# Weights laid out on the host in load order, raw w1 blocks loaded from there, and b2 added by matmuls, in a two-layer transformer block on one core

## The chip, the core and the metric

The kernel runs on one core of a Trainium2 chip. The metric is device time in microseconds (us) of one execution. The core has a matrix engine (TensorE, in profiles PE for matmuls and PEld for weight loads), VectorE (DVE), ScalarE (ACT), GpSimd (POOL) and SyncE (SP), which here only issues DMAs. Every engine takes its instructions in order; they meet through semaphores. Sixteen DMA engines carry all transfers, whichever engine issued them.

## The reference

x has 2048 tokens of 1024 numbers, in bfloat16. Two layers are computed, each an attention part and a feed-forward part with the same weights in both layers:

```python
x = A_x
x = x + _A_ref(_layernorm(x), A_wqkv, A_wo)
x = x + _B_ref(_layernorm(x), B_w1, B_b1, B_w2, B_b2)
x = x + _A_ref(_layernorm(x), A_wqkv, A_wo)
x = x + _B_ref(_layernorm(x), B_w1, B_b1, B_w2, B_b2)
```

_A_ref is attention with 32 heads of 32, in which token s looks at the eight tokens s, s-2, ..., s-14, between a product with wqkv (1024 x 3072) and one with wo (1024 x 1024). _B_ref is h = x w1 + b1 (w1 is 1024 x 3584), h = max(h, 0) squared, out = h w2 + b2 (w2 is 3584 x 1024).

## The kernel before

**Units.** Tokens are sorted into even and odd ones, so that the dilated window becomes a window of eight neighbours. A layer has four blocks of 512 tokens; with two layers these are units u = 0 to 7. For each unit the stages are: SA (load of x, LayerNorm, transposed to xnA), SQ (q, k, v: products `pq` of 8 matmuls of 512 columns each), S2 (window attention on VectorE, with matmuls `lg` and exponentials on ACT), SW (product with wo, `py`, residual `xm`, second LayerNorm to xnB), SF1 (x w1, bias, squared ReLU into `r2`) and SF2 (r2 w2, bias b2, residual, store). Between the layers the residual goes through the DRAM tensor xs, in bfloat16. `build` lists the stages of unit u beside SA, SQ and S2 of unit u + 1.

**The plan.** Nothing is issued as it is listed. Every operation goes into a list with its engine, a guessed duration, a priority and the tiles it reads and writes; `schedule` walks a model of the engines and fixes the order in each engine's queue. Tiles come from slots in size classes (8K: nine slots, among them at most six weight tiles `w`). The operations of `setup` are not in the plan: they are issued first.

**The start.** `setup` makes constants with memsets on VectorE and selects on GpSimd, and loads b1 as b1T (L259) and b2 broadcast to 128 partitions as b2b (L261) by DMAs that GpSimd issues. `build` puts 11 matmuls on constants on TensorE (L1005), which nobody reads. Unit 0's LayerNorm (`ln_first`) runs as statistics on VectorE (L518, L519), two small ACT steps (L522, L523), normalisation on VectorE (L526), transposes on TensorE (L539) and copies out of PSUM on ACT and VectorE (L542). The first products need four x tiles and the k weights, then the q weights: six loads of 1 MB in the order k, k, q, q, v, v. The order of TensorE there is three half products of k on tiles 0 and 1 (L605), one whole one of k, the first one of q (L600), and so on.

**Fast products.** Unit 0 does its feed-forward part plainly (SF1_plain, SF2_plain). Meanwhile it builds what units 1 to 7 use: there both products are cut into 2 x 2 blocks and done with seven block products instead of eight. Some products take sums or differences of blocks of w1 and w2. `keep_w1` and `keep_w2` make those on VectorE and store them in DRAM tensors w1s and tw. The seven products of a step of SF1 take four made blocks (products 3, 5, 6, 7) and three raw ones (1, 2, 4). `copy_w1` copies the raw ones, 21 blocks of 256 KB, from w1 into w1s, DRAM to DRAM, each waiting for one of unit 0's products, so that w1s holds all 49 blocks in the order of use. SF1 then reads w1s in loads of four blocks (1 MB), and treats a raw block's bits as bfloat16.

**b2.** b2 is put into PSUM banks before the products add to them: `seed` lets ACT copy b2b, or the difference b2d of its halves, into a bank (L373): eight banks in unit 0, two X and two Z banks in each of the other units. b2d is made by one VectorE subtraction (L1021) which `build` lists behind S2 of unit 0; it reads nothing that the plan makes, and the plan put it first in VectorE's queue:

```
L586 Memset v
L1021 TensorTensor b2d<-b2b 128x512
L518 BNStats st<-x_110 128x6 x2
```

**Rows in DRAM.** The loads take slices of the weights as the host gave them: wqkv in rows of 2 KB (1024 of 3072 columns), w1 in SF1_plain in rows of 512 B, w2 blocks in SF2 in rows of 1 KB, w2 in SF2_plain in rows of 2 KB.

Of the kernel before, what the change touches and what calls it, by code (L numbers as in the profile page):

```python
# [43 lines left out]
class Buf:  # L44

    __slots__ = ("cls", "tag", "shape", "dt", "left", "slot", "tile", "idx", "seeded")
    count = {}

    def __init__(self, cls, tag, shape, dt):
        self.cls, self.tag, self.shape, self.dt = cls, tag, shape, dt  # L50
        self.left, self.slot, self.tile = 0, None, None
        self.seeded = False
        self.idx = Buf.count[tag] = Buf.count.get(tag, -1) + 1
# [7 lines left out]
class Plan:  # L61
# [45 lines left out]
    def schedule(self):  # L107
# [13 lines left out]
        unset = set(free["ps"])  # L121
# [3 lines left out]
        while left:  # L125
            progress = False
            for e in engs:
# [26 lines left out]
                for b in o.bufs:  # L154
                    if b.slot is None:
                        b.slot = free[b.cls].pop(0)
                        if b.cls == "ps":
                            if b.seeded and b.slot in unset:
                                raise RuntimeError("no product has set the bank of a seeded tile")
                            (unset.add if b.tag == "pt" else unset.discard)(b.slot)  # L160
                        live[b.tag] = live.get(b.tag, 0) + 1
                        placed[b.tag] = placed.get(b.tag, 0) + 1
# [52 lines left out]
class _Kernel:  # L215
    def __init__(self, ctx, tc, x, wqkv, wo, w1, b1, w2, b2, out, n_layers=2):
        self.ctx, self.tc, self.nc = ctx, tc, tc.nc
        self.x, self.wqkv, self.wo, self.w1, self.b1, self.w2, self.b2, self.out = x, wqkv, wo, w1, b1, w2, b2, out
        S, D = x.shape[-2], x.shape[-1]
        self.S, self.D = S, D  # L220
        self.F = w1.shape[-1]
# [13 lines left out]
    def setup(self):  # L235
# [24 lines left out]
        self.b2b = const.tile([128, D], BF, name="b2b")  # L260
        nc.gpsimd.dma_start(self.b2b[:], self.b2.rearrange("(o d) -> o d", o=1).to_broadcast([128, D]))  # L261
        self.b2d = const.tile([128, BLK], F32, name="b2d")

        self.wqkv_v = self.wqkv.rearrange("(kt p) n -> p kt n", p=128)
        self.wo_v = self.wo.rearrange("(p c) n -> p c n", c=self.NCH)
        self.w1_v = self.w1.rearrange("(kt p) n -> p kt n", p=128)
        self.w2_v = self.w2.rearrange("(kt p) n -> p kt n", p=128)
# [4 lines left out]
        self.xs = [tc.dram_tile([self.S, D], BF, name=f"xs{l}") for l in range(self.n_layers - 1)]  # L272
# [4 lines left out]
        self.order1 = self.ffn1_order()  # L277
        self.w1s = [tc.dram_tile([128, min(4, len(self.order1) - i), 4, 256], F16, name=f"w1s{i // 4}") for i in range(0, len(self.order1), 4)]
# [5 lines left out]
        sizes = [("8Q", 3, 8304), ("8K", 9, 8192), ("4K", 12, 4096), ("r2", 1, KF * BLK * 2), ("2K", 8, 2048), ("1K", 9, 1024),  # L284
# [28 lines left out]
    def weights(self, ap, kt, wide=False):  # L313
        b = Buf("8K", "w", [128, 8, 512], BF)
        if wide:
            self.dma(lambda: b[:].rearrange("p (a b) n -> p a (b n)", a=4), lambda: ap, (), [(b, 0)], 1.05, name="w")
        else:
            self.dma(lambda: b[:, :kt, :], lambda: ap, (), [(b, 0)], kt * 0.131, name="w")
        return b

    def w2_block(self, k2, n2):
        h = self.KF // 2
        return self.w2_v[:, k2 * h:(k2 + 1) * h, n2 * BLK:(n2 + 1) * BLK]

    def keep_w2(self, j0, n, w):
# [3 lines left out]
        def raw(k2, n2):  # L329
            return w[:, k2, :n, n2 * BLK:(n2 + 1) * BLK]  # L330
# [9 lines left out]
    def SF2_plain(self, u):  # L340
# [6 lines left out]
        for tl, n2 in banks:  # L347
            self.seed(banks[tl, n2], lambda n2=n2: self.b2b[:, n2 * BLK:(n2 + 1) * BLK], st["ff"][-4])
        for j0 in range(0, h, 2):
            n = min(2, h - j0)  # L350
            w = Buf("8K", "w", [128, 2, 2, 2 * BLK], BF)
            for k2 in range(2):
                self.dma(lambda w=w, k2=k2, n=n: w[:, k2, :n], lambda k2=k2, j0=j0, n=n: self.w2_v[:, k2 * h + j0:k2 * h + j0 + n, :],
                         (), [(w, k2)], n * 0.262, name="w")
            for tl in range(4):
                for n2 in range(2):
                    def fm(tl=tl, n2=n2, w=w, j0=j0, n=n):
                        bank = banks[tl, n2]
                        for k2 in range(2):
                            for j in range(n):  # L360
                                nc.tensor.matmul(bank[:], r2[:, k2 * h + j0 + j, tl * 128:(tl + 1) * 128], w[:, k2, j, n2 * BLK:(n2 + 1) * BLK],  # L361
                                                 start=False, stop=(j0 + n == h and k2 == 1 and j == n - 1), skip_group_check=True)
                    self.pe(2 * n, fm, [(r2, (k2 * h + j0 + j, tl // 2)) for k2 in range(2) for j in range(n)] + [(w, 0), (w, 1)],
# [5 lines left out]
    def seed(self, bank, src, gate):  # L369


        bank.seeded = True
        self.p.add("ACT", act(512), lambda: self.nc.scalar.copy(bank[:], src()), [("b2d", 0)], [(bank, 0)], 0.5, after=[gate], name="seed")  # L373

    def w2_rhs(self, name, half):
# [9 lines left out]
        return self.weights(self.w2_block(k2, n2)[:, half * h:(half + 1) * h, :], h)  # L385

    def ffn1_order(self):

        out = [(0, 1), (1, 1)]
        for a in range(0, self.NDP, 2):  # L390
            steps = [d for d in (a, a + 1) if d < self.NDP]
            then = [(d, 1) for d in (a + 2, a + 3) if d < self.NDP]
            for pr in (5, 6, 2, 7):
                out += [(d, pr) for d in steps]
            out += then
            for pr in (4, 3):
                out += [(d, pr) for d in steps]
        return out

    def copy_w1(self, after):  # L400

        after = iter(after)
        for i, (dp, pr) in enumerate(self.order1):
            if pr in (1, 2, 4):
                gate = next(after)
                m, k = {1: (0, 0), 2: (0, 1), 4: (1, 1)}[pr]
                c0 = m * (self.F // 2) + dp * 256
                self.dma(lambda i=i: self.w1s[i // 4][:, i % 4], lambda k=k, c0=c0: self.w1_v[:, 4 * k:4 * k + 4, c0:c0 + 256],
                         (), [(("w1s", i // 4), i % 4)], 0.3, prio=1e5 + i, after=[gate], name="w1cp", cast=BF)

    def keep_w1(self, dp, w):

        nc, p = self.nc, self.p
        at = {pr: i for i, (d, pr) in enumerate(self.order1) if d == dp}
# [4 lines left out]
        def store(pr, src, r, cast=None):  # L419
            i = at[pr]  # L420
            self.dma(lambda: self.w1s[i // 4][:, i % 4], src, r, [(("w1s", i // 4), i % 4)], 0.26, prio=50.0, name="w1st", cast=cast, lat=4.0)
# [124 lines left out]
    def load_x(self, layer, t, after=(), prio=None, tag="xt"):  # L546
        x = Buf("2K", tag, [128, self.D], BF)
        src, r = (lambda: self.par_tile(self.x_par, t)), ()
        if layer:
            src, r = (lambda: self.xs[layer - 1][t * 128:(t + 1) * 128, :]), [(("xs", layer - 1, t), db) for db in range(2)]  # L550
        self.dma(lambda: x[:], src, r, [(x, 0)], 0.27, prio=-10.0 if prio is None else prio, after=after, name="x")
        return x, lambda: x[:]
# [16 lines left out]
    def SQ(self, u, jobs, order=None, split=0):  # L569
# [6 lines left out]
        cols = {"q": 0, "k": D, "v": 2 * D}  # L576
        offs = {"q": 0, "k": HALO, "v": HALO}
        ws = {}
        for nm in jobs:
            st[nm] = Buf("8Q", nm, [128, NCH, offs[nm] + BLK], F16)  # L580
            ws[nm] = [self.weights(self.wqkv_v[:, 4 * kh:4 * kh + 4, cols[nm]:cols[nm] + D], 8, wide=True) for kh in range(2)]
# [5 lines left out]
            else:  # L587
                src = self.state[u - 1]["halo" + nm]
                p.add("DVE", 0.18, lambda dst=dst, src=src: nc.vector.tensor_copy(dst[:, :, 0:HALO], src[:]),
                      [(src, 0)], [(dst, "h")], -50.0, name="halo")  # L590
        if order is None:
            order = [(nm, c0) for nm in jobs for c0 in range(NCH)]
        for nm, c0 in order:
# [3 lines left out]
            def fm(pq=pq, w=w, c0=c0):  # L597
                for kd in range(KD):
                    wv = w[kd // 4][:].rearrange("p (a b) n -> p a (b n)", a=4)
                    nc.tensor.matmul(pq[:], wv[:, kd % 4, c0:D:8], xnT[:, :, kd, :], start=(kd == 0), stop=(kd == KD - 1))  # L600
            if split:
                def fh(n2, pq=pq, w=w, c0=c0):
                    for kd in range(KD):
                        wv = w[kd // 4][:].rearrange("p (a b) n -> p a (b n)", a=4)
                        nc.tensor.matmul(pq[:, n2 * HB:(n2 + 1) * HB], wv[:, kd % 4, c0:D:8], xnT[:, 2 * n2:2 * n2 + 2, kd, :],  # L605
# [123 lines left out]
    def SW(self, u):  # L729
# [6 lines left out]
        wos = [self.weights(self.wo_v[:, 4 * g:4 * g + 4, :], KD, wide=True) for g in range(2)]  # L736
# [21 lines left out]
    def SF1_plain(self, u):  # L758
        nc, p = self.nc, self.p
        KD, KF, F = self.KD, self.KF, self.F  # L760
# [4 lines left out]
        st["ff"] = []  # L765
        for dp in range(self.NDP):
            w = Buf("8K", "w", [128, 2, 8, 256], BF)
            for m in range(2):
                self.dma(lambda w=w, m=m: w[:, m], lambda m=m, dp=dp: self.w1_v[:, :, m * (F // 2) + dp * 256:m * (F // 2) + (dp + 1) * 256],
                         (), [(w, m)], 0.6, name="w")  # L770
            for m in range(2):
                for a in range(2):
# [18 lines left out]
                    if dp or m:  # L791
                        st["ff"].append(self.pe(8, fm, [(xnT, i) for i in range(4)] + [(w, m)], [(ph, 0), (ph, 1)], name="ph"))
# [8 lines left out]
    def SF1(self, u):  # L801
# [6 lines left out]
        self.ff = st["ff"] = []  # L808
# [11 lines left out]
        for j, (d, pr) in enumerate(self.order1):  # L820
            if j % 4 == 0:
                n = min(4, len(self.order1) - j)
                spare = last and j % 8 == 0
                w = Buf("8Q" if spare else "8K", "wl" if spare else "w", [128, 4, 4, 256], F16)
                self.dma(lambda w=w, n=n: w[:, 0:n], lambda j=j: self.w1s[j // 4][:],
                         [(("w1s", j // 4), i) for i in range(n)], [(w, 0)], n * 0.24, after=[st["attended"]] if spare else (), name="w")
            if d not in steps:
                steps[d] = self.ffn1_step(r2, d)
            steps[d](pr, w, j % 4, *rhs[pr])
# [258 lines left out]
```

## Time and profile before

| | |
|---|---|
| runs | 1220.57, 1220.71, 1224.54 us; median 1220.71 |
| the profiled execution | 1220.71 us, of which the span in the profile 1219.0 us |
| granted TensorE clock over the span | 0.988 |
| DMA packets, bytes, mean rate | 209238, 335.70 MB, 275 GB/s |
| b1T issued, landed after | 1.31 us, 23.2 us |
| b2b issued, landed after | 4.11 us, 21.3 us |
| x tiles of unit 0 issued | 0.81, 1.26, 1.72, 2.20 us, landed after 2.5, 3.6, 4.7, 5.0 us |
| copies L373 on ACT | py 8 at 586 ns, X 14 at 594, Z 14 at 593 |
| DVE xm L752 with a bf16 x tile, L929 with f32 | 690 ns, 685 ns |

How to read the profile: times run from the span's start. A line of the timeline gives start, time taken, engine, line of the kernel, operation, output <- input, shape and count; a bracket gives the idle time of the engine just before it and what ended it. A line of the chain of waits gives start, time, what. A line of the windows gives the stretch, its length, then busy time (and count) of PE, PEld, DVE, ACT and POOL, the granted clock, the share of time that the DMA engines were busy (queues added up, so over 1 is possible) and GB/s. A line of DMA issues gives tensors, queue, count, KB each and the median time from issue to landing.

### The profile page before, as it was taken

How to read it: one execution, taken by the hardware profiler on the slowest of the kernel's cores; microseconds unless marked ns; L12 is line 12 of the kernel's file. 1: busy time of each engine (PE TensorE's matmuls, PEld its weight loads, DVE VectorE, ACT ScalarE, POOL GpSimd, SP SyncE). 2: the span in 40 equal slices, each digit the busy share in tenths (PEclk: the TensorE clock that was granted, in tenths of full speed). 3: DMA queues.
4: the chain of work that ended last, by engine and by line, in shares of the span. 5: the costliest groups of instructions: out<-in, count | busy, mean ns of one | idle time of the engine just before them, and what ended most of it. 6: DMA issues, size and time to landing. Idle time of an engine off the chain costs nothing.

```text
span 1219.0 us, 18015 instructions
## 1 busy us (share of the span) xinstructions
PE 1180.7 (97%) x6887; PEld 741.5 (61%) x6887; DVE 978.5 (80%) x1548; ACT 688.9 (57%) x1274; POOL 4.1 (0%) x10
## 2 busy tenths in 40 slices
PE   1999999999999999999999999999999999989998
PEld 0666644456855578455874568645784556844863
DVE  1399999936999499994999859995899949997562
ACT  0843889149841698218980399506983174724650
POOL 1000000000000000000000000000000000000000
PEclk7899999999999999999999999999999999999999
DMA  9359999966999579987899669996699866787964
GB/s 267 82 197 297 272 333 294 345 218 226 347 321 370 185 243 345 342 290 188 328 299 355 227 226 350 311 360 212 210 336 344 309 191 228 269 299 266 346 235 152
DMA packets 209238, 335.70 MB, mean 275 GB/s; under 512 B 67136, under 2 KB 138048, under 8 KB 196352
## 3 DMA queue, kind: packets, MB, share of 16 engines
q1 hardware_dynamic: 197984, 320.64, 79.4%
q10 hardware_dynamic: 7488, 13.63, 3.2%
q0 software_dynamic: 3680, 0.28, 0.5%
q8 instruction: 54, 0.88, 0.3%
q14 instruction: 32, 0.26, 0.1%
HBM read 284.17 MB, written 42.21 MB: 268 GB/s over the span
## 4 chain that ended last, share of the span: by engine, by line
PE 72%; ACT 14%; DMA 6%; DVE 5%; issue 1%; ACTq 1%; SPq 1%; POOL 0%; POOLq 0%; DVEq 0%
PE pq L600 17%; PE X L923 13%; PE X L867 11%; PE Z L923 7%; PE Z L867 6%; PE py L747 6%; PE py L361 4%; ACT xn L485 3%; PE Y L867 3%; PE Y L923 3%; DMA w<-in_B_w_dram 3%; ACT xn L460 3%; ACT xn L489 3%; DMA b2b<-in_B_b_dram 2%; PE lg L659 1%
## 5 line engine op out<-in xcount | busy, mean ns | idle before, releaser
L600 PE MATMUL pq<-xnA,w 128*128 128x512 f16 x1320 | 289.0, 379 | 0.0
L600 PEld LDWEIGHTS <-w 128*128 128x128 bf16 x1512 | 216.6, 143 | 109.4
L867 PEld LDWEIGHTS <-w 128*128 128x128 f16 (+1 forms) x2544 | 248.8, 98 | 38.9 <-issue 4.1
L704 DVE TENSOR_TENSOR pr<-pb,v 128x2048 f16<-128x2048 f16 x128 | 154.0, 1220 | 0.1
L867 PE MATMUL X<-T,w 128*128 128x256 f16 x1104 | 134.4, 273 | 1.9 <-ACT u L841 1.9
L747 PE MATMUL py<-w,o 128*128 128x512 bf16 x512 | 112.3, 379 | 0.0
L613 ACT CAST k<-pq 128x512 f16<-128x512 f32 x64 | 37.6, 587 | 127.8 <-PE pq L600 126.9
L841 ACT CAST u<-X 128x512 f16<-128x512 f32 x147 | 82.8, 590 | 34.3 <-PE X L867 32.6
L689 ACT ACTIVATE dn<-dn 128x256 f32<-128x256 f32 x16 | 6.7, 416 | 156.7 <-DVE dn L686 156.5
L747 PEld LDWEIGHTS <-o 128*128 128x128 bf16 x512 | 50.0, 98 | 59.6
L707 DVE TENSOR_TENSOR pr<-pr 128x1024 f16<-128x1024 f16 x128 | 85.6, 681 | 0.0
L752 DVE TENSOR_TENSOR xm<-py,xt 128x512 f32<-128x512 f32 x64 | 44.1, 690 | 46.5 <-PE py L747 45.4
L844 DVE TENSOR_TENSOR rr<-u,Z 128x512 f16<-128x512 f16 x98 | 65.4, 681 | 18.8 <-ACT u L841 10.5
L485 ACT ACTIVATE xn<-xm 128x1024 f16<-128x1024 f32 x32 | 33.8, 1056 | 59.6 <-DVE xm L752 56.8
L710 DVE TENSOR_TENSOR pr<-pr 128x512 f16<-128x512 f16 x128 | 51.8, 415 | 0.1
L851 DVE TENSOR_SCALAR rr<-rr,b1T 128x256 f16<-128x256 f16 (+1 forms) x196 | 50.6, 313 | 0.4
L613 ACT CAST v<-pq 128x512 f16<-128x512 f32 x64 | 36.2, 584 | 24.3 <-PE pq L600 20.0
L883 ACT ACTIVATE rr<-X,b1T 128x256 f16<-128x256 f32 x98 | 42.5, 486 | 13.1 <-PE X L867 12.7
L361 PE MATMUL py<-w,r_1341 128*128 128x512 bf16 x224 | 48.7, 379 | 0.0
L779 PE MATMUL ph<-xnB,w 128*128 128x512 f16 x208 | 45.9, 379 | 0.5 <-ACT r L787 0.3
L867 PE MATMUL Y<-xnB,w 128*128 128x256 f16 x376 | 45.9, 273 | 0.0
L867 PE MATMUL Z<-xnB,w 128*128 128x256 f16 x368 | 44.7, 273 | 0.0
(423 smaller groups left out, 1861.2 us busy)
## 6 DMA issues: line engine op xcount, KB each, us to landing
w<-in_A_wqkv_dram SPq DMA_DIRECT2D x48, 1024.0 KB, 7.6
w<-in_B_w_dram SPq DMA_DIRECT2D x42, 896.0 KB, 7.3
w<-in_A_wo_dram SPq DMA_DIRECT2D x16, 1024.0 KB, 6.6
w<-in_B_w_dram SPq DMA_DIRECT2D x28, 512.0 KB, 7.0
w<-tw_79 SPq DMA_DIRECT2D x14, 896.0 KB, 6.6
w<-tw_80 SPq DMA_DIRECT2D x14, 896.0 KB, 9.3
w<-tw_81 SPq DMA_DIRECT2D x14, 896.0 KB, 7.7
w<-tw_82 SPq DMA_DIRECT2D x14, 896.0 KB, 8.9
```

Source lines behind the costliest of these rows:

```text
L361: nc.tensor.matmul(bank[:], r2[:, k2 * h + j0 + j, tl * 128:(tl + 1) * 128], w[:, k2, j, n2 * BLK:(n2 + 1) * BLK], start=False, stop=(j0 + ...
L485: nc.scalar.activation(out=xn[:], in_=xv(), func=ACTF.Identity, accum_out=s1())
L600: nc.tensor.matmul(pq[:], wv[:, kd % 4, c0:D:8], xnT[:, :, kd, :], start=(kd == 0), stop=(kd == KD - 1))
L613: p.add("ACT", act(512), lambda dst=dst, c0=c0, off=off, pq=pq: nc.scalar.copy(dst[:, c0, off:off + BLK], pq[:]), [(pq, 0), (pq, 1)], [(ds ...
L704: nc.vector.tensor_tensor(pr[:], pb[:], _win_ap(v[:, c, :], HALO + hb * HB, HB), ALU.mult)
L707: nc.vector.tensor_tensor(pr[:, 0:4, :], pr[:, 0:4, :], pr[:, 4:8, :], ALU.add)
L710: nc.vector.tensor_tensor(pr[:, 0:2, :], pr[:, 0:2, :], pr[:, 2:4, :], ALU.add)
L747: nc.tensor.matmul(py[:], o[:, c, tl * 128:(tl + 1) * 128], wos[c // 4][:].rearrange("p (a b) n -> p a (b n)", a=4)[:, c % 4, db * 512:(db ...
L841: p.add("ACT", act(512), lambda: nc.scalar.copy(us[i][:], X[:]), [(X, 0)], [(us[i], 0)], 1.0, name="u")
L844: p.add("DVE", dve(512, False), lambda: nc.vector.tensor_tensor(r[:, :, m, :], us[i][:], bank[:], ALU.add), [(us[i], 0), (bank, 0)], [(r, ...
L867: nc.tensor.matmul(bank[:, a, :], lw[:, k, a * 128:(a + 1) * 128], rhs(k), start=(start and k == 0 and a == 0), stop=(k == 3), skip_group_ ...
L923: nc.tensor.matmul(banks[q][:], left(jj, q), w[:, j, :], start=(start and jj == 0), stop=(jj == h - 1), skip_group_check=True)
```

## The change

- **Layout.** The host reorders wqkv, w1 and w2 so that each load finds one run per partition: 8 KB for wqkv, 4 KB for w1 in SF1_plain, 7 KB for the w2 blocks in SF2 (the loads of SF2_plain keep 2 KB rows). `_layout` does this.
- **Raw w1 blocks.** The host also gives B_w1r, the 21 raw blocks in order of use. `copy_w1` is gone; w1s holds the 28 made blocks. SF1 reads two streams, raw and made, each in loads of four blocks, so two w tiles are in use at a time.
- **b2.** b2b, b2d and `seed` are gone. b2's halves lie in rows 32 and 0 of a tile b2r that is zero elsewhere; `pick` tiles have one row of ones each (pickd: ones in one row, minus ones in the other). One matmul pick x b2r of 512 columns starts each bank that was seeded.
- **Beside these.** The residual between the layers is stored and loaded in float32 (xs, xo, xt), with x tiles moved to the 4K class (14 slots instead of 12) and xo to 2K (1K has 7 slots instead of 9). The unused input B_x is dropped.

The core of the diff:

```diff
-        self.b2b = const.tile([128, D], BF, name="b2b")
-        nc.gpsimd.dma_start(self.b2b[:], self.b2.rearrange("(o d) -> o d", o=1).to_broadcast([128, D]))
-        self.b2d = const.tile([128, BLK], F32, name="b2d")
+        self.b2r = const.tile([128, BLK], BF, name="b2r")
+        nc.vector.memset(self.b2r[:], 0.0)
+        for n2, row in enumerate((32, 0)):
+            nc.gpsimd.dma_start(self.b2r[row:row + 1, :], self.b2.rearrange("(o d) -> o d", o=1)[:, n2 * BLK:(n2 + 1) * BLK])
+        self.pick = {}
+        for n2, row in enumerate((32, 0)):
+            t = self.pick[n2] = const.tile([128, 128], BF, name=f"pick{n2}")
+            nc.vector.memset(t[:], 1.0)
+            nc.gpsimd.affine_select(out=t[:], in_=t[:], pattern=[[0, 128]], compare_op=ALU.is_equal,
+                                    fill=0.0, base=-row, channel_multiplier=1)
+        t = self.pick["d"] = const.tile([128, 128], BF, name="pickd")
+        nc.vector.tensor_tensor(t[:], self.pick[1][:], self.pick[0][:], ALU.subtract)
...
-    def seed(self, bank, src, gate):
-        bank.seeded = True
-        self.p.add("ACT", act(512), lambda: self.nc.scalar.copy(bank[:], src()), [("b2d", 0)], [(bank, 0)], 0.5, after=[gate], name="seed")
+    def add_b2(self, bank, n2, start):
+        self.nc.tensor.matmul(bank[:], self.pick[n2][:], self.b2r[:], start=start, stop=False, skip_group_check=True)
...
-        self.p.add("DVE", 0.35, lambda: self.nc.vector.tensor_tensor(self.b2d[:], self.b2b[:, BLK:], self.b2b[:, :BLK], ALU.subtract),
-                   (), [("b2d", 0)], self.nxt(), name="b2d")
...
-                    self.copy_w1([op for op in self.p.ops if op.eng == "PE" and op.name in ("pq", "py")][-24:])
...
-            ws[nm] = [self.weights(self.wqkv_v[:, 4 * kh:4 * kh + 4, cols[nm]:cols[nm] + D], 8, wide=True) for kh in range(2)]
+            ws[nm] = [self.weights(self.wqkv["qkv".index(nm), kh], 8) for kh in range(2)]
...
-        return self.weights(self.w2_block(k2, n2)[:, half * h:(half + 1) * h, :], h)
+        return self.weights(self.w2[k2, n2, :, half * h:(half + 1) * h, :], h)
...
-        for j, (d, pr) in enumerate(self.order1):
+        at, ws = [0, 0], [None, None]
+        for d, pr in self.order1:
+            raw = pr in (1, 2, 4)
+            j, at[raw] = at[raw], at[raw] + 1
             if j % 4 == 0:
-                n = min(4, len(self.order1) - j)
+                n = min(4, len(self.kept1 if raw else self.made1) - j)
...
+                src = self.w1r[j // 4, :, 0:n] if raw else self.w1s[j // 4][:]
...
-        xo = Buf("1K", "xo", [128, BLK], BF)
+        final = layer == self.n_layers - 1
+        xo = Buf("2K", "xo", [128, BLK], BF if final else F32)
...
+def _layout(inputs):
+
+    import numpy as np
+    wqkv, w1, w2 = (np.asarray(inputs[n]) for n in ("A_wqkv", "B_w1", "B_w2"))
+    D, F = w1.shape
+    KD, KF, ND = D // 128, F // 128, F // 512
+    a = wqkv.reshape(2, KD // 2, 128, 3, 128, 4, 2)
+    wqkv = a.transpose(3, 0, 2, 5, 1, 6, 4).reshape(3, 2, 128, KD, D // 2)
+    b = w1.reshape(KD, 128, 2, ND, 256).transpose(2, 3, 1, 0, 4)
+    kept = [o for o in ffn1_order(ND) if o[1] in (1, 2, 4)]
+    w1r = np.zeros(((len(kept) + 3) // 4, 128, 4, 4, 256), w1.dtype)
+    for i, (d, pr) in enumerate(kept):
+        m, k = {1: (0, 0), 2: (0, 1), 4: (1, 1)}[pr]
+        w1r[i // 4, :, i % 4] = b[m, d, :, 4 * k:4 * k + 4]
+    w2 = w2.reshape(2, KF // 2, 128, 2, D // 2).transpose(0, 3, 2, 1, 4)
+    return dict(inputs, A_wqkv=wqkv, B_w1=b, B_w1r=w1r, B_w2=w2)
```

In VectorE's queue of the changed kernel the subtraction for pickd stands behind the statistics of unit 0's four x tiles; TensorE's order up to the first q product is as before.

## The prediction

> **What bounds the kernel now.** I read four views, in this order: busy time, the chain of waits, the timeline of the first 60 us, and the windows of 20 us over the whole span. Busy time and the costliest groups say which engine has no room:
>
> ```profile
> PE 1180.7 (97%) x6887; PEld 741.5 (61%) x6887; DVE 978.5 (80%) x1548; ACT 688.9 (57%) x1274; POOL 4.1 (0%) x10
> ...
> L600 PE MATMUL pq<-xnA,w 128*128 128x512 f16 x1320 | 289.0, 379 | 0.0
> ```
>
> TensorE is busy 1180.7 of 1219.0 us. The 379 ns of a matmul is its latency, not its price: in a row they start every 289.0 us / 1320 = 0.219 us, and the chain has "PE pq x64" in 13.81 us, 0.216 us each. I use 0.216 us for 512 columns and, from "PE Z L867 x32" in 3.49 us, 0.109 us for 256. So the span is that stream plus 1219.0 - 1180.7 = 38.3 us in which TensorE is idle. The chain and the timeline say where most of those are:
>
> ```profile
> 4.11 21.34 DMA b2b<-in_B_b_dram
> 34.19 1.71 PE pq L605 x8
> ```
>
> ```profile
> 5.34 4.43 PE L1005 MATMUL pk<-grp 128*128 128x512 f16 x10 [5.34 <-POOL grp L249]
> ...
> 25.47 0.69 DVE L1021 TENSOR_TENSOR b2d<-b2b 128x512 f32<-128x512 bf16 x1 [24.05 <-DMA b2b<-in_B_b_dram]
> 26.08 1.28 DVE L518 BATCH_NORM_STATS2 st<-x_110 128x6 f32<-128x512 bf16 x2
> ...
> 33.99 1.91 PE L605 MATMUL pq<-xnA,w 128*128 128x256 f16 x8
> ```
>
> The reader is to see a queue blocked by an instruction nobody needs yet. b2d (L1021) stands at the head of VectorE's queue and waits until 25.47 us for the broadcast of b2, which lies in the software DMA queue behind the load of b1 (4-byte elements). Behind b2d stand the first LayerNorm's statistics, though their x_110 was issued at 0.81 us and landed 2.5 us later. TensorE's first product waits for them and starts at 33.99 us. b2d's own reader comes only after 340 us. The windows show the rest:
>
> ```profile
> 0.00:20.00 20.00, 4.43 (x10) 1.34 (x10) 0.51 (x6) 1.28 (x1) 4.07 (x10) 0.83 1.11 281
> 20.00:40.00 20.00, 9.34 (x65) 7.49 (x65) 9.24 (x19) 8.43 (x19) 0.00 (x0) 0.58 0.39 139
> 40.00:60.00 20.00, 20.00 (x106) 13.84 (x105) 6.46 (x6) 17.69 (x38) 0.00 (x0) 1.00 0.40 107
> ...
> 1060.00:1080.00 20.00, 16.50 (x100) 10.01 (x99) 17.83 (x31) 10.81 (x16) 0.00 (x0) 0.91 0.81 279
> ...
> 1200.00:1220.00 20.00, 15.46 (x72) 6.83 (x70) 4.15 (x6) 0.00 (x0) 0.00 (x0) 0.95 0.12 41
> ```
>
> TensorE's column is the first busy time: it lacks 15.6 + 10.7 = 26.3 us before 40 us, 3.5 us in 1060:1080, 3.5 us behind the last product, and some 5 us in all the other windows together. A gain can come from the first 40 us and hardly from elsewhere; whatever is added to TensorE after them is paid in full.
>
> **The start.** b2d and b2b go. In their place VectorE gets, ahead of the first statistics, one memset of 128x512 and two of 128x128 (the 128x128 memset of ident took 0.17 us, so some 0.6 us in all; the last memset now ends at 1.4 us, then at 2.0, before x_110 lands at 0.81 + 2.5 = 3.3). The subtraction that makes pickd waits for two more selects on GpSimd. In the new order of VectorE's queue it stands behind the statistics of all four x tiles, and behind it wait the copy of a transposed tile and the normalisation of the fourth tile, for which TensorE waits in turn. GpSimd's queue now ends its selects at 4.73 + 0.56 = 5.3 us; one more DMA issue (0.61 for b2b's) and two more selects (0.30 to 0.34) bring it to 6.6 us. VectorE comes to pickd at about 3.4 + 6 = 9.4 us, so it waits for nothing. Without that cover, were GpSimd held up, its lateness would be paid one for one.
>
> From the first statistics to the first product takes 33.99 - 26.08 = 7.9 us, and to the copy of the last transposed tile (0.69 us from 36.79) 11.4 us. From 3.4 us this gives 11.3 and 14.8 us. The fourth tile landed at 2.20 + 5.0 = 7.2 us and its statistics come 5.1 us behind the first, at 8.5: x is no limit. The ten matmuls of L1005 hold the transposes until 9.8 us, which leaves the last tile near 15. The weights are next late. Loads of wqkv, in order k, k, q, q, v, v, are six of 1 MB:
>
> ```profile
> w<-in_A_wqkv_dram SPq DMA_DIRECT2D x6, 1024.0 KB, 14.3
> ```
>
> In the trace's list of packets the last packet of x ends at 8.6 us, and those of the first four weight loads at 11.8, 15.0, 18.1 and 21.3 us: 3.17 us each, landing some 0.8 us later (k at 15.7, q at 22.2). The new rows are 8 KB instead of 2 KB. A 2048-byte packet took 84 ns (median), an 8192-byte one 309, against 4 x 84 = 336: a factor 0.92, 2.9 us a load. k then lands at 8.6 + 2 x 2.9 + 0.8 = 15.2 us, q at 21.1. In TensorE's order, the same as before here, three half products (24 x 0.109) and one whole one (8 x 0.216) stand ahead of the first that needs q: 4.35 us, so TensorE is ready for q at 19.6 and waits to 21.1. Before, that product began at 38.49 + 8 x 0.216 = 40.2 us. Gain 19.1 us. Bounds: if TensorE's clock is at half for those products, as in the ten matmuls of L1005 (4.43 us, 0.43 each), they take twice 4.35 us, q begins at 15.2 + 8.7 = 23.9, gain 16; if b2's absent packets speed the loads by 0.8 us more, gain 20. v lands 6 us behind q, long before its turn 26 us later. All that follows moves with it: VectorE, ACT and the DMAs were idle in that stretch as well (DMA share 0.40 in 40:60).
>
> The Trainium skill, DMA: Bandwidth & Descriptors, Specifications, puts the least transfer for line rate at 512 B, which speaks against the layout: none of these rows was shorter. The packets here disagree: 512 B took 27 ns (19 B/ns), 8192 B 309 ns (26.5 B/ns). By the rule q would land at 22.2 us as before and the sum below would be 1.1 us higher.
>
> **b2 on TensorE.** Each of the 36 ACT copies at L373 (8 in the first unit, four in each of seven) becomes a matmul of 512 columns: 36 x 0.216 = +7.8 us, nothing covering it, as TensorE is full there. Its weight load hides (98 ns against 216). The copies' 36 x 0.59 us on ACT were off the chain but for single pieces (X L923 waited 0.4 us for one); I take 0.4 us back. That is the whole of what the removed copies give.
>
> **Loads after the start.** Packet medians over 16 engines: 48 wqkv loads save 32 x 84 - 8 x 309 ns = 0.22 us of DMA time each; 42 of w2 (1 KB rows at 46 ns to 7 KB at 274) 0.38 us; 14 of w1 (512 B at 27 to 4 KB at 159, as b2b's) 0.46 us. The 21 copies of w1 into the scratch go: 21 x 32 x 27 ns = 18 us. Sum about -51 us. The diff also makes the residual between the layers f32: 32 loads grow by 8 x (159 - 84) ns = 0.6 us, 32 stores by 0.3 us, +29 us. TensorE lost only 0.5 us in 120:200 where the copies stood in SP's queue, so taking them out gives at most that. The engines see no price of f32: xm from a f32 tile took 685 ns against 690 from bf16, ACT's pass over f32 1056 against 1073. Two streams of w1 blocks, raw and made, keep two of the six w buffers open instead of one. No row prices that: between -10 us (every idle piece after 40 us but the tail, with the slow clock at 1073 us) and +8 us (they double). The DMA balance is near zero within a unit (-3.6 us for the rows, +2.4 or +4.8 for f32), so I take -0.6, near zero.
>
> **Sum.** 1219.0 - 19.1 + 7.8 - 0.4 - 0.6 = 1206.7 us of span. The run with that profile took 1220.71, 1.7 more, and is the median of the three: forecast 1208.4.
>
> **Rivals.** *The start's wait only changes its name* (0.07): GpSimd's second software DMA waits until b1 has drained at 24.5 us, so the selects end near 25.5 and pickd holds VectorE as b2d did. The tile copy behind it would run at 26.2 instead of 33.02: gain 6.8, total 1220.7. For it: b1's 23.2 us to landing. Against: b2b was issued at 4.11, in 0.61 us, right behind b1. *The prefetch shrinks* (0.07, the side slower): in the FFN stages of seven units DMA share is at 1.0 or over, and Y L923 already waited 3.1 us for a w2 block, with 1.8 us of slow clock after it. If the second open buffer makes that happen once in each unit, 7 x 4.9 = 34 us come on top: 1243. It outweighs the gain from 12.3 us, 1.8 us a unit. Against: the same bytes in cheaper packets. *The loads cease to be late* (0.10): the idle pieces after 40 us go, another 9 us: 1199. *The forecast* (0.76), own range 1203 to 1214. That the layout doesn't do what it says costs 1.1 us, inside it.
>
> **Numbers.** Range 1200 to 1217: it leaves out the slower rival, most of the moved wait and a few of the 1199 case. Measurement tells 0.5%, 6.1 us, from no change. Faster (below 1214.6): 0.74 of the forecast and 0.10, 0.84. Slower: 0.06. The same: the rest, 0.10.
>
> **What would show it.** The first statistics at 3 to 4 us and no long wait on VectorE; the first product that needs q at about 21 us, behind a wait for its load; 36 more matmuls and none of L373 on ACT; the windows from 40 us on as full as now. I am wrong if VectorE or the k weights hold the first product past 20 us, or if TensorE loses over 2 us in each FFN stage.

## The result and the profile after

The changed kernel took 1204.92 us (median of 4 runs, 1203.83 to 1208.04) against 1221.84 us of the kernel before beside it: ratio 0.9863, 95% interval 0.9837 to 0.9889. The profiled execution has a span of 1203.4 us, 15.6 us less than before.

Busy time first:

```profile
PE 1184.1 (98%) x6923; PEld 673.9 (56%) x6923; DVE 978.4 (81%) x1551; ACT 670.4 (56%) x1238; POOL 5.0 (0%) x13
...
L572 PE MATMUL pq<-xnA,w 128*128 128x512 f16 x1320 | 289.0, 379 | 0.0
```

TensorE has 36 matmuls more and is as full as it was; ACT lost its 36 copies. The products of wqkv take the same 289.0 us. Their weight loads fell from 143 to 98 ns, now that the columns lie side by side (with the columns strided again, in the run with wqkv in the old rows, they took 144 ns), and nothing waited for them: they ran beside matmuls of 216 ns.

The chain of waits (start, time, what) has no b2 at its head any more:

```profile
4.13 10.64 DMA w<-in_A_wqkv_dram
17.62 8.64 PE pq L572 x40
```

The timeline of the start, first VectorE, then TensorE:

```profile
3.45 1.29 DVE L486 BATCH_NORM_STATS2 st<-x_113 128x6 f32<-128x512 bf16 x2 [1.47 <-DMA x_113<-in_A_x_dram]
...
10.54 0.22 DVE L265 TENSOR_TENSOR pickd<-pick_80,pick_77 128x128 bf16<-128x128 bf16 x1
```

```profile
12.16 0.61 PE L576 MATMUL pq<-xnA,w 128*128 128x256 f16 x4 [0.71 <-DMA w<-in_A_wqkv_dram]
14.81 0.61 PE L576 MATMUL pq<-xnA,w 128*128 128x256 f16 x4 [2.04 <-DMA w<-in_A_wqkv_dram]
...
15.71 1.91 PE L576 MATMUL pq<-xnA,w 128*128 128x256 f16 x16
17.45 8.80 PE L572 MATMUL pq<-xnA,w 128*128 128x512 f16 x40
```

The first statistics run at 3.45 us instead of 26.08 and wait for x alone. The first product starts at 12.16 us with the first of the two k loads: four of its eight matmuls, then a wait of 2.04 us for the second load. The whole products (x40) begin at 17.45 us instead of 38.49, 21.0 us earlier, and from there TensorE goes on without a break. The windows that answer to those shown of before:

```profile
0.00:20.00 20.00, 11.95 (x79) 6.92 (x79) 10.16 (x28) 10.23 (x22) 5.00 (x13) 1.00 1.01 312
20.00:40.00 20.00, 20.00 (x106) 10.27 (x106) 7.49 (x7) 18.04 (x39) 0.00 (x0) 1.00 0.86 211
...
1040.00:1060.00 20.00, 16.94 (x118) 11.59 (x117) 19.77 (x38) 10.77 (x16) 0.00 (x0) 0.95 0.83 303
```

The idle piece of the last unit but one is still there (3.06 us in 1040:1060, 3.50 us in 1060:1080 before).

**Where the 15.6 us come from.** The starts of all matmuls stand in the trace. From the start of the first whole product I add up what the gaps between starts exceed 0.216 us (512 columns) or 0.109 us (256), counting excesses over 0.05 us. Called "lost" below:

| run (profiled execution) | span | first whole product | lost after it |
|---|---|---|---|
| before | 1219.0 | 38.49 | 13.7 |
| changed | 1203.4 | 17.45 | 11.1 |
| changed, again | 1208.2 | 17.52 | 15.9 |

The sum for the first two: -21.0 (start) + 36 x 0.216 = 7.8 (b2) - 2.6 (lost) + 0.2 (behind the last product) = -15.6 us. The third row is the same program: what is lost differs by 4.8 us from one execution to the next, 3.5 of them in waits for w2 blocks (4.5 us in all in the first, 8.0 in the second). So the start and the matmuls are effects, and the -2.6 us of this pair lies inside the scatter.

### The profile page after: what moved, and what is told of

Same layout as the page of the kernel before. It is cut to its first block, busy times and chain, and to the rows that moved or that the text cites. A ratio compares the mean times of both kernels' runs of the same rounds, so it can differ in the third digit from the quotient of the medians.

```text
span 1203.4 us, 18070 instructions
## 1 busy us (share of the span) xinstructions
PE 1184.1 (98%) x6923; PEld 673.9 (56%) x6923; DVE 978.4 (81%) x1551; ACT 670.4 (56%) x1238; POOL 5.0 (0%) x13
## 4 chain that ended last, share of the span: by engine, by line
PE 68%; DVE 13%; ACT 12%; DMA 3%; issue 2%; ACTq 1%; SPq 0%; DVEq 0%
PE X L897 14%; PE pq L572 12%; PE X L839 11%; PE Z L897 7%; PE Z L839 6%; PE py L356 4%; PE Y L897 3%; PE py L718 3%; ACT xn L428 3%; ACT xn L457 3%; PE ph L749 3%; PE Y L839 3%; ACT xn L453 3%; PE lg L630 1%; DMA w<-in_B_w_dram 1%
## 5 line engine op out<-in xcount | busy, mean ns | idle before, releaser
L572 PE MATMUL pq<-xnA,w 128*128 128x512 f16 x1320 | 289.0, 379 | 0.0
L572 PEld LDWEIGHTS <-w 128*128 128x128 bf16 x1512 | 147.8, 98 | 176.9 <-DMA w<-in_A_wqkv_dram 0.3
L839 PE MATMUL X<-T,w 128*128 128x256 f16 x1072 | 131.4, 273 | 0.8 <-ACT u L814 0.8
L817 DVE TENSOR_TENSOR rr<-u,Z 128x512 f16<-128x512 f16 x98 | 65.4, 682 | 17.8 <-ACT u L814 10.2
L839 PE MATMUL Z<-xnB,w 128*128 128x256 f16 x384 | 48.0, 272 | 1.6 <-DVE rr L817 1.6
L839 PE MATMUL X<-xnB,w 128*128 128x256 f16 x376 | 45.6, 273 | 0.0
```

Of the source, the lines that this page charges most:

```text
L572: nc.tensor.matmul(pq[:], wv(w, c0, kd), xnT[:, :, kd, :], start=(kd == 0), stop=(kd == KD - 1))
L817: p.add("DVE", dve(512, False), lambda: nc.vector.tensor_tensor(r[:, :, m, :], us[i][:], bank[:], ALU.add), [(us[i], 0), (bank, 0)], [(r, ...
L839: nc.tensor.matmul(bank[:, a, :], w[:, wi, k, a * 128:(a + 1) * 128], rhs(k), start=(start and k == 0 and a == 0), stop=(k == 3), skip_gro ...
```

## The experiments

Each ran in several rounds beside the kernel before; ratios are to that kernel, with 95% intervals.

**b2d late, nothing else.** The kernel before, with the head of VectorE's queue cleared:

```diff
-                   (), [("b2d", 0)], self.nxt(), name="b2d")
+                   (), [("b2d", 0)], self.nxt(), after=[self.state[0]["attended"]], name="b2d")
```

> The kernel before, with one thing changed: the subtraction that makes b2d is put behind unit 0's attention in VectorE's queue; rows, seeds and copies stay. Theory (a blocked queue at the start is the gain): first statistics at 3.4 us, the first q product at 22.2 us when q's second load with 2 KB rows lands, against 40.2: 18 us less, span about 1201, ratio to before about 0.985. Rival (the laid out rows are the gain): the start stays near 34 us or moves by a few us only, span 1214 or more, ratio above 0.995.

Measured: 1203.02 us, ratio 0.9851 (0.9833 to 0.9869), span 1201.1 us.

```profile
3.49 1.29 DVE L518 BATCH_NORM_STATS2 st<-x 128x6 f32<-128x512 bf16 x2 [2.07 <-DMA x<-in_A_x_dram]
```

```profile
15.95 0.66 PE L605 MATMUL pq<-xnA,w 128*128 128x256 f16 x4 [2.52 <-DMA w<-in_A_wqkv_dram]
...
18.64 8.80 PE L600 MATMUL pq<-xnA,w 128*128 128x512 f16 x40
```

One argument does what the whole change does: the first whole product moves from 38.49 to 18.64 us, 19.9 us. The rival (the rows bring it) falls. The first product of q began where it was expected, at 18.64 + 16 x 0.216 = 22.1 us (22.2 expected). The expected gain of 18 us was low because its base was wrong: in the kernel before, that product began at 41.9 us and not at 40.2, as shown below under the prediction.

**Seeds back.** The changed kernel with b2 put into the banks by ACT again:

```diff
-                        if j0 == 0:
-                            self.add_b2(bank, n2, True)
...
+        for tl, n2 in banks:
+            self.seed(banks[tl, n2], lambda n2=n2: self.b2b[:, n2 * BLK:(n2 + 1) * BLK], st["ff"][-4])
...
+                   (), [("b2d", 0)], self.nxt(), after=[self.state[0]["attended"]], name="b2d")
```

> The changed kernel with b2 put into the banks by ScalarE copies again (b2b, b2d, 36 copies, no matmuls for b2), b2d made behind unit 0's attention, one 4K slot less for space. Theory (36 matmuls of 0.216 us are paid in full): span 1203.4 - 7.8 = 1195.6, ratio about 0.980. Rival (they hide, or the copies cost the same through waits): span within 2 us of 1203.4.

Measured: 1199.48 us, ratio 0.9815 (0.9799 to 0.9831), span 1197.9. It ran a second time:

> The run with seeds by ScalarE again, as it is, on the same chip as the one before it: span 1196 to 1198, ratio 0.980 to 0.983.

Measured: 1198.40 us, ratio 0.9801 (0.9784 to 0.9818), span 1197.1. Beside the changed kernel's 0.9863 and 0.9869 the copies are cheaper than the matmuls by about 0.6%. The first of the two spans is 2.3 us above what was expected: its start lost 1.7 us (19.14 instead of 17.45 us) to TensorE's clock, shown further down, and 0.7 us more was lost later.

**Seeds back, b2d first.** The same without the added argument, so that b2d's subtraction leads VectorE's queue.

> As the run before it, but with b2d's subtraction at the head of VectorE's queue as in the kernel before; rows, raw blocks and f32 residual are those of the changed kernel. Theory (blocked queue): the first q product near 40 us again, span 1195.6 + 21 = 1216.6, 2 to 3 us under the kernel before. Rival (rows are the gain): span near 1200.

Measured: 1222.75 us, ratio 1.0005 (0.9993 to 1.0017), span 1219.0.

```profile
26.96 0.69 DVE L994 TENSOR_TENSOR b2d<-b2b 128x512 f32<-128x512 bf16 x1 [25.54 <-DMA b2b<-in_B_b_dram]
```

All of the new layout, the raw blocks from the host and the f32 residual are in this kernel, and it is as fast as the kernel before. The blocked queue decides. The expected 2 to 3 us of gain were lost at the start: b2b landed 1.5 us later than before (26.96 against 25.47 at b2d), as b1's load took 25.0 us instead of 23.2 beside 8 KB packets, and the first whole product began at 40.76 instead of 38.49 us; 2.5 us less was lost after it.

**b2 twice.** The changed kernel with

```diff
+        self.nc.tensor.matmul(bank[:], self.zero[:], self.b2r[:], start=False, stop=False, skip_group_check=True)
```

behind each matmul for b2.

> The changed kernel as it is, on the chip of the three runs that follow, as their yardstick: ratio to before 0.984 to 0.989, span 1203 to 1205.

> The changed kernel with a second matmul of 512 columns behind each of the 36 for b2, which adds zeros. Theory (each is paid in full, 0.216 us): 7.8 us slower than the changed kernel, span 1211.2. Rival (part of them falls into waits or hides): under 4 us slower.

Measured: the changed kernel again 1207.66 us, ratio 0.9869 (0.9849 to 0.9889), span 1208.2, which is 3 us over what was expected; with 72 matmuls 1212.88 us, ratio 0.9908 (0.9893 to 0.9924), span 1211.2. With none, 36 and 72 of them the medians are 1198.4 and 1199.5, 1204.9 and 1207.7, 1212.9 us: steps of about 7 us for 36 x 0.216 = 7.8. The step from the run beside it alone, 5.2 us, with the scatter of 3 us, would not settle it; the three levels together do. That the span of 1211.2 us is just the expected one is luck: against the first profile of the changed kernel, this execution began its whole products 1.7 us later (19.13 us, the granted clock was about half from 15 to 19 us) and lost 1.7 us less after that.

**bf16 residual.** The changed kernel with

```diff
-        self.xs = [tc.dram_tile([self.S, D], F32, name=f"xs{l}") for l in range(self.n_layers - 1)]
+        self.xs = [tc.dram_tile([self.S, D], BF, name=f"xs{l}") for l in range(self.n_layers - 1)]
...
-        xo = Buf("2K", "xo", [128, BLK], BF if final else F32)
+        xo = Buf("2K", "xo", [128, BLK], BF)
```

> The changed kernel with the residual between the layers in bfloat16 again (stores of 128 KB, loads of 256 KB). Theory (f32 is bought from idle DMA time): span within 1.5 us of 1203.4. Rival (29 us more of DMA time make weights late in the feed-forward stages): span 3 us or more below 1203.4.

Measured: 1206.78 us, ratio 0.9872 (0.9851 to 0.9893), span 1203.9. The f32 residual costs nothing that can be told.

**Raw blocks copied.** The changed kernel, with the 21 raw blocks first copied into a scratch:

```diff
+            self.dma(lambda i=i: self.w1k[i // 4][:, i % 4], lambda i=i: self.w1r[i // 4, :, i % 4],
+                     (), [(("w1k", i // 4), i % 4)], 0.3, prio=1e5 + i, after=[gate], name="w1cp")
...
-                src = self.w1r[j // 4, :, 0:n] if raw else self.w1s[j // 4][:]
+                src = self.w1k[j // 4][:] if raw else self.w1s[j // 4][:]
```

> The changed kernel, but with the 21 raw w1 blocks copied from B_w1r into a DRAM scratch by SP during unit 0, as before, and read from that scratch. Theory (the copies stood beside a full TensorE and cost nothing): within 1.5 us of the changed kernel. Rival (copies in SP's queue make unit 0's weights late): slower by 4 us or more, with TensorE waiting for DMA between 100 and 200 us.

Measured: 1203.66 us, ratio 0.9836 (0.9816 to 0.9856), span 1200.3: not slower, and 4 us faster than the changed kernel beside it. To see whether that was an effect, it ran again, and once with the seeds by ACT:

> The changed kernel with the raw blocks copied, a second time. If the copies gain: ratio 0.982 to 0.984 again. If that was scatter: 0.985 to 0.987, as the changed kernel.

> Seeds by ScalarE, new rows, b2d late, and the raw blocks copied into a scratch as in the run with copies. If the copies really gain (the run with them was 4 us faster than the changed kernel beside it), 2 to 4 us below the runs with seeds back: span 1193 to 1195, ratio about 0.978. If that was scatter: within 1.5 us of them, ratio 0.980 to 0.982.

Measured: 1204.97 us, ratio 0.9865 (0.9848 to 0.9881); with the seeds 1198.98 us, ratio 0.9820 (0.9806 to 0.9833). Scatter: with copies 0.9836 and 0.9865 against 0.9863 and 0.9869, with seeds 0.9820 against 0.9815 and 0.9801. Leaving the copies out gains nothing that can be told.

**wqkv in the old rows.** The changed kernel with

```diff
-            ws[nm] = [self.weights(self.wqkv["qkv".index(nm), kh], 8) for kh in range(2)]
+            ws[nm] = [self.wide(self.wqkv.rearrange("(kt p) n -> p kt n", p=128)[:, 4 * kh:4 * kh + 4, "qkv".index(nm) * D:("qkv".index(nm) + 1) * D]) for kh in range(2)]
```

> The changed kernel, but with wqkv as the host gave it: rows of 2 KB, weight columns strided by 8 in SBUF. Theory: the four first loads take 3.17 us each instead of 2.6, the first whole product begins at 18.6 us as in the run with b2d late, against 17.45: 1.2 us slower, and nothing later. Rival (short rows and strided weight loads cost throughout): 4 us or more slower.

Measured: 1208.26 us, ratio 0.9871 (0.9851 to 0.9890), beside the changed kernel's 0.9869. The first whole product began at 21.10 us instead of 18.6. The rows account for the expected part: the second half of the first product began at 15.96 us, as in the run with b2d late (15.95). The rest is TensorE's clock, which was granted at 0.50 from 15 to 20 us; the sixteen matmuls before the first whole product took 3.62 us instead of 1.92:

```profile
17.68 3.62 PE L581 MATMUL pq<-xnA,w 128*128 128x256 f16 x16
```

The 1.2 us expected of the rows cannot be told in the time of several runs: 1 to 2 us are under their scatter.

**b1 and b2 loaded late.** Seeds by ACT and the new rows, and the bias loads held back by a memset of b1T in VectorE's queue:

```diff
+        m = self.p.add("DVE", 0.1, lambda: nc.vector.memset(self.b1T[:], 0.0), (), [("b1T", 0)], -50.0, after=[gate], name="b1z")
+        o = self.p.add("POOL", 1.7, f1, (), [("b1T", 0)], 0.0, after=[m], lat=25.0, name="b1")
+        self.p.add("POOL", 0.6, f2, (), [("b2b", 0)], 1.0, after=[o], lat=25.0, name="b2")
```

> The run with seeds by ScalarE and the new rows, and in addition the loads of b1 and b2 issued only when VectorE has begun the first window product (a memset of b1T in VectorE's queue holds GpSimd's DMA back), so that b1's 4-byte packets no longer run beside the first weights. Theory: x and the k weights land about 1.3 us earlier, q's by 2; the first whole product begins at 16 us instead of 17.5 to 19; span 1194 to 1197, ratio about 0.979, better than both kernels. Rival (the first LayerNorm's steps hold the start then, or the clock is at half): within 1 us of the run without the late loads, 1197.9.

Measured: 1199.55 us, ratio 0.9815 (0.9798 to 0.9832), span 1199.2; no better than without. The weights did land earlier: the second half of the first product began at 13.74 us, against 14.81 in the changed kernel and 14.51 in the run without the late loads beside it, so by 0.8 us in the closest pair where 1.3 were expected. But the first whole product began at 18.03 us, against 17.15 in that pair. The window of 15 to 17 us says why; the column behind POOL's is the granted clock. First this run, then the changed kernel:

```profile
15.00:17.00 2.00, 2.00 (x14) 1.57 (x13) 0.69 (x1) 1.87 (x6) 0.00 (x0) 0.50 1.00 418
```

```profile
15.00:17.00 2.00, 2.00 (x24) 1.84 (x23) 0.69 (x1) 1.87 (x6) 0.00 (x0) 1.00 1.07 398
```

TensorE was granted half its clock and did 14 matmuls where the changed kernel did 24. The theory's DMA part holds in kind, with less than the expected size, and its gain was eaten by the clock, which is the second case of the rival: from 13.74 to 18.03 us took 4.3 us, the same work in the run beside it 2.6.

**The best version.** The new rows with the seeds on ACT and b2d behind unit 0's attention: 1199.48 and 1198.40 us, about 0.981 of the kernel before and 0.994 of the changed one. Against b2d late alone (0.9851) the rows and what goes with them bring about 0.4%; which part of them does was not separated. So the 1.4% of the whole change is 1.5% from the cleared queue and about 0.4% from the rows and what goes with them, less about 0.6% for b2's matmuls.

## Why the prediction was right

**The bound and the blocked queue.** Right, and shown both ways: b2d late alone gives 0.9851; b2d first, with seeds by ACT and all the rest of the change, gives 1.0005. pickd did not take the wait over: it ran at 10.54 us without any (forecast 9.4), as GpSimd's selects ended at 6.2 us (forecast 6.6).

**The size of the start.** 19.1 us forecast, 21.0 measured, through two terms. First, the prediction let a product begin when both of its loads had landed. The waits are by load: the first half of the first product ran at 12.16 us on one load, so that q's first product needed its second load only half a product after its start; it began at 17.45 + 8 x 0.216 = 19.2 us, without a wait, against 21.1 forecast (its second load landed at 20.0 us, when its first four matmuls were done). Second, a load of 8 KB rows was put at 2.9 us, by the medians of packets of the whole run (309 against 4 x 84 ns). In the trace's list of packets the first four loads took 2.61 us each in the changed kernel, and 3.17 with 2 KB rows: beside b1's 4-byte packets the 2 KB packets had a median of 98 ns, not 84, and the 8 KB packets 324, not 309, and 324 / (4 x 98) = 0.83 agrees with 2.61 / 3.17 = 0.82. The price should have come from that stretch. b2's absence, which the prediction allowed 0.8 us, had no part: with b2b loaded again and 8 KB rows the four loads took 2.61 us as well. The prediction's times for the ends of packets are all 0.3 us late (the first four loads end at 11.5, 14.7, 17.8 and 21.0 us in the trace), which leaves their distance as it is.

The Trainium skill, DMA: Bandwidth & Descriptors, Specifications, with line rate from 512 B on, would have the loads equal; in this stretch they were not (3.17 against 2.61 us a MB), so the measurement decides, though several runs cannot tell the microsecond it is worth at the start.

One reading under this term was wrong, in the account of the start ahead of the prediction as well. In the kernel before, two whole products of k, not one, run ahead of the first of q; in the changed kernel it is one, so TensorE's order there is not as before. ACT's copies of the finished products show it, first before, then changed:

```profile
40.42 0.59 ACT L613 CAST k<-pq 128x512 f16<-128x512 f32 x1 [0.45 <-PE pq L600]
42.19 0.57 ACT L613 CAST k<-pq 128x512 f16<-128x512 f32 x1
43.87 0.59 ACT L613 CAST q<-pq 128x512 f16<-128x512 f32 x1
```

```profile
19.38 0.59 ACT L584 CAST k<-pq 128x512 f16<-128x512 f32 x1 [1.94 <-PE pq L572]
21.16 0.57 ACT L584 CAST q<-pq 128x512 f16<-128x512 f32 x1
```

So 40.2 us is where TensorE's second whole product began before, and the first one of q began at 38.49 + 16 x 0.216 = 41.9 us. The 21.0 us do not depend on this: they are the distance between the first whole products, and equally between the second ones.

**b2 on TensorE.** +7.8 us forecast and confirmed by three levels of matmul count. Its price exceeds what the ACT copies cost: with them TensorE waited 1.1 us in all for a seed (three waits of X), and the prediction took 0.4 us for that.

**The later loads.** -0.6 us forecast, -2.6 in the pair of profiles. The term is right in kind, near zero: two executions of the changed kernel lost 11.1 and 15.9 us, and copies, f32 residual and rows of wqkv each made no difference that can be told. Two open w buffers did not starve the products either: no wait for a w1 block stands among TensorE's waits in the changed kernel. Of the 3.3 us between the forecast span of 1206.7 us and the 1203.4 measured, 1.9 lie in the start and 1.6 in what was lost later, less 0.2 behind the last product. The 1.6 lie inside the scatter, as the other profile of the same kernel has 1208.2 us; a forecast closer than that would have been luck.

**The rivals.** The wait that only changes its name and the smaller prefetch did not come; the case of loads that cease to be late did not either: TensorE still waited 4.5 and 8.0 us for w2 blocks in two executions of the changed kernel, against 4.7 before. For the smaller prefetch the prediction took a DMA share of 1.0 or over in the FFN stages of all seven units; in the last unit but one it was 0.68 to 0.81 before (1040 to 1120 us), and there the longest wait for a w2 block stood.

## What to carry to other kernels

Look at the head of each in-order queue: an instruction that nobody needs soon, but that waits for a slow DMA, stops all that stands behind it, and moving it costs one argument. Where TensorE is full for the whole span, do not move work onto it from an engine with room: each matmul of 512 columns was worth 0.216 us here. And before a layout is credited for a gain that came with it, put the layout in alone.

## What was not expected

TensorE's clock at the start decides up to 2.5 us (21.10 against 18.64 us for the first whole product, both with 2 KB rows), and executions with nearly the same start differ. The prediction had half the clock as a bound of its start, with a gain of 16 us, but not that it would come in one execution and not in the next. The kernel with seeds back, run twice, did the same sixteen matmuls in 3.58 us and in 1.91 us:

```profile
15.75 3.58 PE L574 MATMUL pq<-xnA,w 128*128 128x256 f16 x16
```

```profile
15.40 1.91 PE L574 MATMUL pq<-xnA,w 128*128 128x256 f16 x16
```

The granted clock was 0.50 from 17 to 19 us in the first and 1.00 in the second. TensorE had waited 1.1 and 2.0 us ahead of these products in the first, 0.4 and 1.9 us in the second, and 0.71 and 2.04 us in the changed kernel, which did the same sixteen in 1.91 us. So the length of these waits alone does not tell which it will be.

In the run with late bias loads TensorE's constant matmuls ended earlier, the transposes stood alone, and the clock was at 0.50 from 12 to 17 us; that the one is the reason for the other is not shown. The Trainium skill, TensorE: Matmul & The Clock Gate, Part 1, says that the window which watches TensorE's activity runs freely, so that the point of change varies from run to run. These runs agree with it, with 1.91 against 3.58 us for the same sixteen matmuls.
